# Strided sparse attention with a feed-forward block on one core: scores of two heads or slots from one full-row matmul with a block-diagonal query tile

## The chip, the core and the metric

One of the eight cores of a Trainium2 chip runs the whole program. The metric is the device time in microseconds of one execution, as the median of several runs; smaller is better. The engines named below are PE (TensorE, the matrix engine), ACT (ScalarE), DVE (VectorE), POOL (GpSimd, here only the issuer of loads) and SP (here only the issuer of stores). PSUM is the memory that matmuls write, in eight banks; SBUF is the memory that everything else is in.

## What is computed

For 8 batches of 8 heads, 576 positions and head size 64, attention with two fixed sparse masks, and then a feed-forward layer with a squared ReLU over all 4608 tokens:

```python
scores = scale * np.matmul(q, k.transpose(0, 1, 3, 2))
mask_local   = (rel >= 0) & (rel < 32)                                        # heads 0 to 3
mask_strided = (rel >= 0) & (pos[None, :] % 32 == pos[:, None] % 32)          # heads 4 to 7
attn = softmax(np.where(masks, scores, -1e9));   x = np.matmul(attn, v)
h = x @ w_in;  r = np.maximum(h, 0.0)
out = (s * (r * r) + b) @ w_out            # x: 4608 x 512, w_in: 512 x 2048, w_out: 2048 x 512
```

Since the masks are sparse, a local head needs only six blocks of 96 queries against 128 keys, and a strided head only eight blocks ("slots") of 72 queries against 72 keys.

## The kernel before, in words

**Attention of a batch.** `load_qk` and `load_v` (lines 100 to 136) load a batch through POOL's queue. The heads are worked on in four pairs, m = 0 and 1 local, m = 2 and 3 strided. `pair_steps` (line 149) makes five lists of steps for a pair, each step with one matmul:

- T (`trans`, line 160): transposes of q and then of k into a PSUM tile `ps_t` (two buffers). The last transpose of each is followed by a copy on ACT into SBUF, 128 rows by 576 columns (line 180 for local pairs, 185 for strided). In the copy, two heads (local) or two neighbouring slots of a head (strided) lie one above the other: rows 0 to 63 and rows 64 to 127.
- S (`score`, line 196): the scores. Each matmul contracts over 64 rows, one head or slot, and gives keys by 96 (or 72) queries: 12 matmuls for a local pair and 16 for a strided one. Neighbouring steps use the upper and the lower 64 rows in turn. Three of them fill a PSUM tile `ps_s` (two buffers); then ACT takes the exponential of 288 columns (line 211) and DVE multiplies by the mask (line 216).
- A0 and A1 (`av`, line 227): probabilities times values for the first and the second head, 6 (local) or 8 (strided) matmuls each. A column of ones beside v gives the sums; after 6 (local) or 4 (strided) matmuls DVE takes reciprocals (line 240) and scales into `x_nat` (line 242). The PSUM tile `ps_a` has one buffer, so the next group of A steps has to wait until line 242 has read it.
- X (`xtrans`, line 252): transposes of `x_nat` into `xT`, the input of the feed-forward layer.

`batch_steps` (line 274) puts the lists of the four pairs in one sequence, in phases: in a phase the T steps of a pair stand in alternating halves with the S steps of the pair before it, followed by the A0 steps of the pair before that, X of the pair before that, and A1. X of the last pair is kept apart.

**Feed-forward of a block.** A block is 512 tokens, and there are nine (T = 0 to 8). FF1 is 64 matmuls of 512 columns into `ps_f` (three buffers); after every fourth, ACT takes the ReLU into `u` (line 307) and DVE squares it into `gT` (line 308). FF2 is another 64 matmuls; after every 16th DVE makes the output (line 322) and SP stores it. In block 0 a group of 16 matmuls (line 340) that needs `w_out` stands between FF1 and FF2.

**The order.** It is written out by hand and every engine works in program order. Batch 0 runs alone. Then block T carries the attention of batch T + 1 among its own 128 matmuls: step i of the sequence stands ahead of feed-forward matmul number int(i * 112 / len(seq)), and X of the last pair stands at numbers 118 to 120. Blocks 0 to 6 carry attention, blocks 7 and 8 none. The two lines that place the steps are:

```python
for i, f in enumerate(seq):
    at.setdefault(int(i * 112 / len(seq)), []).append(f)
```

Of the kernel before, what the change touches and what calls it, by code (L numbers as in the profile page):

```python
# [9 lines left out]
FP16 = mybir.dt.float16  # L10
FP32 = mybir.dt.float32
AF = mybir.ActivationFunctionType
ALU = mybir.AluOpType
# [3 lines left out]
def kernel(  # L17
# [11 lines left out]
    nc = tc.nc  # L29
    B, H, S, D = q.shape  # L30
# [3 lines left out]
    scale = 1.0 / float(np.sqrt(D))  # L34
# [6 lines left out]
    LQ, LT, LPAD = 96, 6, 32  # L41
    SQ, ST = 72, 8
# [13 lines left out]
    const = ctx.enter_context(tc.tile_pool(name="consts", bufs=1))  # L56
    inp = ctx.enter_context(tc.tile_pool(name="inp", bufs=2))
    qkp = ctx.enter_context(tc.tile_pool(name="qkp", bufs=2))
    ptp = ctx.enter_context(tc.tile_pool(name="ptp", bufs=8))
# [4 lines left out]
    op = ctx.enter_context(tc.tile_pool(name="op", bufs=3))  # L64
    psum = ctx.enter_context(tc.tile_pool(name="psum", bufs=1, space=bass.MemoryType.PSUM))
# [11 lines left out]
    v_loc = [const.tile([128, 4, LT, D + 1], FP16, name=f"v_loc{i}") for i in range(NV)]  # L77
    v_str = [const.tile([SQ, 4, ST, D + 1], FP16, name=f"v_str{i}") for i in range(NV)]
    kT_loc = [const.tile([128, LPAD + S], FP16, name=f"kT_loc{i}") for i in range(2)]
    xT = [const.tile([128, NTOK], FP16, name=f"xT{i}") for i in range(4)]  # L80

    sched = ctx.enter_context(tc.manual_schedule())
# [11 lines left out]
        nc.vector.memset(v_str[i][:, :, :, D:D + 1], 1.0)  # L94
    for i in range(2):
        nc.vector.memset(kT_loc[i][:, 0:LPAD], 0.0)

    loaded = {}

# [49 lines left out]
    def pair_steps(b, m):  # L149

        loc = m < 2
        nq, nt = (LQ, LT) if loc else (SQ, ST)
        sfx = "l" if loc else "s"
        mm = m % 2
        half = nt // 2
        nk = 128 if loc else SQ
        st = {}
        T, SS, A0, A1, X = [], [], [], [], []

        def trans(name, j):  # L160
            def f():
                if j == 0:
                    st["p" + name] = psum.tile([128, S], FP16, tag="t", bufs=2, name="ps_t")
                ps = st["p" + name]

                src = (paired[b, name][:, mm, j] if loc else
                       loaded[b][name + sfx][:, 2 * mm + j // 4,
                                             (j % 4) * 128:(j % 4) * 128 + 128])
                nc.tensor.matmul(  # L169
                    out=ps[:, nq * j:nq * j + nq], lhsT=src,  # L170
                    rhs=ident[0:nq, 0:nq], is_transpose=True)
                if j == nt - 1:
                    if loc:
                        if name == "q":
                            st["q"] = qkp.tile([128, S], FP16, tag="qTl", name="qTl")
                            dst = st["q"]
                        else:
                            st["k"] = kT_loc[mm]
                            dst = st["k"][:, LPAD:LPAD + S]
                        nc.scalar.copy(  # L180
                            out=dst.rearrange("d (p j) -> d p j", j=nt),
                            in_=ps.rearrange("d (j p) -> d p j", j=nt))
                    else:
                        st[name] = qkp.tile([128, S], FP16, tag=name + "Ts", name=name + "Ts")
                        nc.scalar.copy(out=st[name], in_=ps)  # L185
            return f

        for name in ("q", "k"):
            for j in range(nt):
                T.append(trans(name, j))  # L190

        def grp(j):

            return (j // half, j % half) if loc else (j % 2, j // 2)

        def score(e, j):
            def f():
                g, i = grp(j)
                if i == 0:
                    st["s", e, g] = psum.tile([128, 3 * LQ], FP32, tag="s", bufs=2, name="ps_s")  # L200
                ps = st["s", e, g]
                c = i * nq
                r0, at = (64 * e, j * nq) if loc else (64 * (j % 2), (4 * e + j // 2) * nq)
                rr = slice(r0, r0 + 64)
                nc.tensor.matmul(  # L205
                    out=ps[0:nk, c:c + nq], lhsT=st["k"][rr, at:at + nk],
                    rhs=st["q"][rr, at:at + nq])
                if i == half - 1:
                    pt = ptp.tile([128, half, nq], FP16, tag="pt" + sfx, name="pt")
                    st["pt", e, g] = pt  # L210
                    nc.scalar.activation(  # L211
                        out=pt[0:nk].rearrange("k t c -> k (t c)"),
                        in_=ps[0:nk, 0:half * nq], func=AF.Exp, scale=scale)
                    mask = (mask_loc if loc else mask_str)[:, None, :].to_broadcast(
                        [nk, half, nq])
                    nc.vector.tensor_tensor(out=pt[0:nk], in0=pt[0:nk], in1=mask, op=ALU.mult)  # L216
            return f

        for a in range(2):
            for j in range(half):  # L220
                for c in range(2):
                    SS.append(score(c, a * half + j) if loc else score(a, 2 * j + c))

        per = nt if loc else nt // 2
        vt = (v_loc if loc else v_str)[b % NV]

        def av(e, j):
            def f():
                if j == 0 and e == 0:
                    st["x"] = xnp.tile([nq, nt, 128], FP16, tag="x" + sfx, name="x_nat")  # L230
                if j % per == 0:
                    st["a"] = psum.tile([128, 6, D + 1], FP32, tag="a", bufs=1, name="ps_a")
                ps = st["a"]
                nc.tensor.matmul(  # L234
                    out=ps[0:nq, j % per, :],
                    lhsT=st["pt", e, grp(j)[0]][0:nk, grp(j)[1], :],
                    rhs=vt[0:nk, 2 * mm + e, j, :])
                if j % per == per - 1:
                    rec = recp.tile([128, 6, 1], FP32, tag="rec", name="rec")
                    nc.vector.reciprocal(out=rec[0:nq, 0:per], in_=ps[0:nq, 0:per, D:D + 1])  # L240
                    j0 = j - per + 1
                    nc.vector.tensor_tensor(  # L242
                        out=st["x"][:, j0:j0 + per, 64 * e:64 * e + 64],
                        in0=ps[0:nq, 0:per, 0:D],
                        in1=rec[0:nq, 0:per].to_broadcast([nq, per, D]), op=ALU.mult)
            return f

        for j in range(nt):
            A0.append(av(0, j))
            A1.append(av(1, j))  # L250

        def xtrans(j):
            def f():
                if j == 0:
                    st["px"] = psum.tile([128, S], FP16, tag="t", bufs=2, name="ps_t")
                ps = st["px"]
                nc.tensor.matmul(  # L257
                    out=ps[:, nq * j:nq * j + nq], lhsT=st["x"][:, j, :],
                    rhs=ident[0:nq, 0:nq], is_transpose=True)
                if j == nt - 1:  # L260
                    dst = xT[m][:, b * S:(b + 1) * S]
                    if loc:
                        nc.vector.tensor_copy(out=dst, in_=ps)
                    else:
                        nc.scalar.copy(  # L265
                            out=dst.rearrange("d (p j) -> d p j", j=nt),
                            in_=ps.rearrange("d (j p) -> d p j", j=nt))
            return f

        for j in range(nt):  # L270
            X.append(xtrans(j))
        return T, SS, A0, A1, X

    def batch_steps(b):

        P = [pair_steps(b, m) for m in range(4)]
        seq = []
        for ph in range(6):
            Tn = P[ph][0] if ph < 4 else []
            Sn = P[ph - 1][1] if 0 <= ph - 1 < 4 else []  # L280
            seq += Sn[:len(Sn) // 2] + Tn[:len(Tn) // 2] + Sn[len(Sn) // 2:] + Tn[len(Tn) // 2:]
            if 0 <= ph - 2 < 4:
                seq += P[ph - 2][2]
            if 0 <= ph - 3 < 4:
                seq += P[ph - 3][4]
            if 0 <= ph - 2 < 4:
                seq += P[ph - 2][3]
        return seq, P[3][4]
# [67 lines left out]
    for T in range(NBLK):  # L356
        F = ffn_steps(T)
        at = {}
# [46 lines left out]
```

## Time and profile before

| | us |
|---|---|
| median of 3 runs (lowest to highest) | 461.65 (460.33 to 464.23) |
| the profiled execution, its own time | 465.23 |
| its span, first to last instruction | 463.5 |
| PE busy in the span | 393.1 |
| ACT busy | 177.7 |
| DVE busy | 198.6 |

The profiled execution is 3.6 us longer than the median of the runs, and 1.7 us of its time lie outside the span. In the trace a PE instruction's duration covers the filling and emptying of the array too, and matmuls overlap, so what one costs the engine is read from the distance between starts and not from its duration.

### The profile page before, as it was taken

The page shows a single profiled execution, that of the slowest core. Times are in us where ns is not written, and L with a number is a line of the kernel's source. Part 1 is how long each engine was busy: PE and PEld are TensorE (multiplying, and loading weights), DVE is VectorE, ACT ScalarE, POOL GpSimd, SP SyncE. Part 2 cuts the span into 40 slices and gives each one's busy share as a digit, 9 for nine tenths or more (in the row PEclk, how much of TensorE's full clock was granted, in tenths as well). Part 3 has the DMA queues.
Part 4 walks back from the last instruction along what each step waited for, and adds up shares of the span by engine and source line. Part 5 has one row for each costly group of instructions (what it writes and reads, how often), then busy time and mean ns, then how long its engine had stood idle before and what let it go on. Part 6 is the DMA issues. An engine that isn't in the chain of part 4 may idle for free.

```text
span 463.5 us, 6912 instructions
## 1 busy us (share of the span) xinstructions
PE 393.1 (85%) x2736; PEld 194.7 (42%) x2736; DVE 198.6 (43%) x557; ACT 177.7 (38%) x354; POOL 100.1 (22%) x137
## 2 busy tenths in 40 slices
PE   1848799788978989788978898888969797999995
PEld 0633344344434444344434343444434343444442
DVE  1552434444453444434444444434444355352431
ACT  2614651065503751065414651166305541260530
POOL 6736436510244012510252022400000000000000
PEclk9999999899999999899999999899999999899999
DMA  8999999960567114850458025700001001101101
GB/s 108 93 204 100 164 156 141 88 103 1 60 75 87 32 25 60 68 102 0 61 75 119 1 30 67 82 24 1 24 24 45 1 0 47 45 2 46 47 23 69
DMA packets 72516, 28.99 MB, mean 63 GB/s; under 512 B 53028, under 2 KB 67876, under 8 KB 72484
## 3 DMA queue, kind: packets, MB, share of 16 engines
q0 software_dynamic: 66640, 19.04, 44.1%
q1 hardware_dynamic: 5844, 9.51, 5.6%
q8 instruction: 21, 0.34, 0.3%
q14 instruction: 11, 0.09, 0.1%
HBM read 38.08 MB, written 9.44 MB: 103 GB/s over the span
## 4 chain that ended last, share of the span: by engine, by line
PE 71%; DVE 9%; ACT 7%; DMA 6%; issue 3%; POOL 2%; ACTq 0%; POOLq 0%
PE ps_f L302 27%; PE ps_f L317 26%; PE ps_s L205 9%; DVE x_nat L242 5%; PE ps_a L234 4%; ACT u L307 4%; DMA kl<-in_k_dram 3%; PE ps_t L169 3%; DMA qs<-in_q_dram 2%; ACT kT_loc L180 2%; DVE rec L240 2%; PE ps_t L257 1%; DVE o L322 1%; DVE gT L308 1%; ACT kTs L185 1%
## 5 line engine op out<-in xcount | busy, mean ns | idle before, releaser
L302 PE MATMUL ps_f<-xT,w_in_sb 128*128 128x512 f16 x576 | 178.2, 388 | 0.0
L317 PE MATMUL ps_f<-w_out_sb,gT 128*128 128x512 f16 x576 | 166.9, 393 | 0.0
L307 ACT ACTIVATE u<-ps_f 128x512 f16<-128x512 f32 x144 | 86.0, 597 | 72.9 <-PE ps_f L302 72.3
L308 DVE TENSOR_TENSOR gT<-u 128x512 f16<-128x512 f16 x144 | 61.3, 426 | 109.2 <-ACT u L307 109.2
L317 PEld LDWEIGHTS <-gT 128*128 128x128 f16 x576 | 58.0, 102 | 39.1 <-issue 4.3
L234 PEld LDWEIGHTS <-pt 72*72 72x72 f16 (+1 forms) x448 | 44.1, 127 | 71.3 <-DVE x_nat L242 58.3
L211 ACT ACTIVATE pt<-ps_s 72x288 f16<-72x288 f32 (+1 forms) x128 | 48.2, 407 | 59.8 <-PE ps_s L205 58.4
L302 PEld LDWEIGHTS <-w_in_sb 128*128 128x128 f16 x576 | 56.8, 99 | 33.4 <-issue 0.6
L234 PE MATMUL ps_a<-v_str,pt 72*72 72x65 f16 x256 | 39.1, 211 | 29.1 <-DVE x_nat L242 28.8
L265 ACT COPY xT<-ps_t 128x576 f16<-128x576 f16 x16 | 10.2, 639 | 108.6 <-PE ps_t L257 108.6
L242 DVE TENSOR_TENSOR x_nat<-ps_a,rec 72x256 f16<-72x256 f32 (+1 forms) x96 | 44.6, 465 | 3.3
L322 DVE SCALAR_TENSOR_TENSOR o<-ps_f,s_sb,bcs 128x512 f32<-128x512 f32 x36 | 26.9, 747 | 37.1 <-PE ps_f L317 37.1
L134 POOL DMA_DIRECT2D v_str<-in_v_dram x32 | 28.0, 875 | 65.5 <-PE ps_a L234 45.4
L240 DVE RECIPROCAL rec<-ps_a 72x4 f32<-72x4 f32 (+1 forms) x96 | 17.4, 181 | 53.3 <-PE ps_a L234 52.5
L234 PE MATMUL ps_a<-v_loc,pt 128*96 128x65 f16 x192 | 27.3, 209 | 13.2 <-DVE x_nat L242 13.2
L205 PE MATMUL ps_s<-qTl,kT_loc 64*128 64x96 f16 x192 | 26.3, 221 | 11.3 <-ACT kT_loc L180 11.3
L205 PE MATMUL ps_s<-qTs,kTs 64*72 64x72 f16 x256 | 34.4, 222 | 0.8 <-ACT pt L211 0.5
L205 PEld LDWEIGHTS <-kTs 64*72 64x72 f16 x256 | 16.6, 112 | 33.1 <-issue 32.8
L257 PE MATMUL ps_t<-ident,x_nat 72*128 72x72 f16 (+1 forms) x224 | 29.9, 215 | 0.5 <-DVE x_nat L242 0.5
L133 POOL DMA_DIRECT2D v_loc<-in_v_dram x32 | 28.7, 898 | 6.1 <-DVE x_nat L242 2.3
L216 DVE TENSOR_TENSOR pt<-pt,mask_str 72x288 f16<-72x288 f16 x64 | 19.0, 304 | 25.2 <-ACT pt L211 25.1
L205 PEld LDWEIGHTS <-kT_loc 64*128 64x128 f16 x192 | 11.6, 95 | 40.2 <-issue 23.5
(37 smaller groups left out, 251.3 us busy)
## 6 DMA issues: line engine op xcount, KB each, us to landing
out_dram<-o SPq DMA_DIRECT2D x36, 256.0 KB, 2.1
v_loc<-in_v_dram POOLq DMA_DIRECT2D x32, 80.0 KB, 3.5
ql<-in_q_dram POOLq DMA_DIRECT2D x8, 288.0 KB, 5.3
kl<-in_k_dram POOLq DMA_DIRECT2D x8, 288.0 KB, 6.2
qs<-in_q_dram POOLq DMA_DIRECT2D x8, 288.0 KB, 6.6
ks<-in_k_dram POOLq DMA_DIRECT2D x8, 288.0 KB, 8.1
v_str<-in_v_dram POOLq DMA_DIRECT2D x32, 72.0 KB, 3.6
w_in_sb<-in_moe_w_in_dram POOLq DMA_DIRECT2D x4, 512.0 KB, 9.7
```

The source lines that it names most:

```text
L133: nc.gpsimd.dma_start(out=vl[:, h, 1:LT, 0:D], in_=src)
L134: nc.gpsimd.dma_start(out=vs[:, h, :, 0:D], in_=v[b, 4 + h].rearrange("(p j) d -> p j d", j=ST))
L205: nc.tensor.matmul(out=ps[0:nk, c:c + nq], lhsT=st["k"][rr, at:at + nk], rhs=st["q"][rr, at:at + nq])
L211: nc.scalar.activation(out=pt[0:nk].rearrange("k t c -> k (t c)"), in_=ps[0:nk, 0:half * nq], func=AF.Exp, scale=scale)
L234: nc.tensor.matmul(out=ps[0:nq, j % per, :], lhsT=st["pt", e, grp(j)[0]][0:nk, grp(j)[1], :], rhs=vt[0:nk, 2 * mm + e, j, :])
L242: nc.vector.tensor_tensor(out=st["x"][:, j0:j0 + per, 64 * e:64 * e + 64], in0=ps[0:nq, 0:per, 0:D], in1=rec[0:nq, 0:per].to_broadcast([nq ...
L257: nc.tensor.matmul(out=ps[:, nq * j:nq * j + nq], lhsT=st["x"][:, j, :], rhs=ident[0:nq, 0:nq], is_transpose=True)
L302: nc.tensor.matmul(out=st["h"], lhsT=w_in_sb[:, ct, ft * 128:(ft + 1) * 128], rhs=xT[ct][:, tok0:tok0 + PS], start=(ct == 0), stop=(ct == 3))
L307: nc.scalar.activation(out=u, in_=st["h"], func=AF.Relu)
L308: nc.vector.tensor_tensor(out=st["g"][:, ft, :], in0=u, in1=u, op=ALU.mult)
L317: nc.tensor.matmul(out=st["o"], lhsT=st["g"][:, ft, ts * 128:(ts + 1) * 128], rhs=w_out_sb[:, ft, :], start=(ft == 0), stop=(ft == NFT - 1))
L322: nc.vector.scalar_tensor_tensor(out=o, in0=st["o"], scalar=s_sb[:, 0:1], in1=bcs, op0=ALU.mult, op1=ALU.add)
```

## The change

The q copy of a pair no longer goes into one dense tile. It goes into a tile `qD_loc` or `qD_str` that holds, for each block of queries, twice as many columns: in the first half of the columns only rows 0 to 63 are filled, in the second half only rows 64 to 127, and the rest is zero. These tiles are zeroed once, at the start, by DVE, and the zeros are never overwritten. ACT copies the upper 64 rows and DVE the lower 64. A score step is now one matmul over all 128 rows: 192 columns (local) or 144 columns (strided), and it gives the scores of both heads or slots. There are half as many score steps, 6 or 8 to a pair; two (local) or three (strided) of them fill a `ps_s` tile, so the exponential and the mask now work on 384, 432 or (last group of a strided pair) 288 columns. The k copies, the transposes and the A and X steps are as before, except for where A finds its probabilities.

```diff
+    qD_loc = [const.tile([128, LT, 2, LQ], FP16, name=f"qD_loc{i}") for i in range(2)]
+    qD_str = [const.tile([128, ST, 2, SQ], FP16, name=f"qD_str{i}") for i in range(2)]
...
     for i in range(2):
         nc.vector.memset(kT_loc[i][:, 0:LPAD], 0.0)
+        nc.vector.memset(qD_loc[i], 0.0)
+        nc.vector.memset(qD_str[i], 0.0)
...
-                        if name == "q":
-                            st["q"] = qkp.tile([128, S], FP16, tag="qTl", name="qTl")
-                            dst = st["q"]
...
-                        st[name] = qkp.tile([128, S], FP16, tag=name + "Ts", name=name + "Ts")
-                        nc.scalar.copy(out=st[name], in_=ps)
+                    if name == "q":
+                        qD = (qD_loc if loc else qD_str)[mm]
+                        st["q"] = qD
+                        for e, copy in ((0, nc.scalar.copy), (1, nc.vector.tensor_copy)):
+                            hs = slice(64 * e, 64 * e + 64)
+                            if loc:
+                                copy(out=qD[hs, :, e, :].rearrange("d t (p j) -> d t p j", j=nt),
+                                     in_=ps[hs].rearrange("d (j t p) -> d t p j", j=nt, t=nt))
+                            else:
+                                copy(out=qD[hs, :, e, :],
+                                     in_=ps[hs].rearrange("d (j p) -> d j p", j=nt))
...
-                r0, at = (64 * e, j * nq) if loc else (64 * (j % 2), (4 * e + j // 2) * nq)
-                rr = slice(r0, r0 + 64)
-                nc.tensor.matmul(
-                    out=ps[0:nk, c:c + nq], lhsT=st["k"][rr, at:at + nk],
-                    rhs=st["q"][rr, at:at + nq])
-                if i == half - 1:
+        per_s = 2 if loc else 3
+
+        def score(i):
+            def f():
+                g, n = i // per_s, min(per_s, nt - i // per_s * per_s)
+                if i % per_s == 0:
+                    st["s", g] = psum.tile([128, 3 * 2 * SQ], FP32, tag="s", bufs=2, name="ps_s")
...
+                c = i % per_s * 2 * nq
+                nc.tensor.matmul(
+                    out=ps[0:nk, c:c + 2 * nq], lhsT=st["k"][:, i * nq:i * nq + nk],
+                    rhs=st["q"][:, i].rearrange("d e c -> d (e c)"))
+                if i % per_s == n - 1:
...
-        for a in range(2):
-            for j in range(half):
-                for c in range(2):
-                    SS.append(score(c, a * half + j) if loc else score(a, 2 * j + c))
+        for i in range(nt):
+            SS.append(score(i))
```

The placed sequence of a batch has 160 steps in place of 188, so the other steps move too: 1.43 steps stand ahead of each of the first 112 feed-forward matmuls of a block in place of 1.68.

On PE, block 3, in FF1, where the first scores of batch 4 follow the k transposes of its first pair (`ps_f` rows are feed-forward, `ps_s` rows scores); before:

```order
L302 LDWEIGHTS w_in_sb
L302 MATMUL ps_f<-xT_102,w_in_sb 128x512
L205 LDWEIGHTS kT_loc_98
L205 MATMUL ps_s<-qTl,kT_loc_98 128x96
L205 LDWEIGHTS kT_loc_98
L205 MATMUL ps_s<-qTl,kT_loc_98 128x96
L302 LDWEIGHTS w_in_sb
L302 MATMUL ps_f<-xT_103,w_in_sb 128x512
```

The same place after the change, where line 313 is the FF1 matmul and line 213 the score:

```order
L313 LDWEIGHTS w_in_sb
L313 MATMUL ps_f<-xT_107,w_in_sb 128x512
L213 LDWEIGHTS kT_loc_98
L213 MATMUL ps_s<-qD_loc_100,kT_loc_98 128x192
L313 LDWEIGHTS w_in_sb
L313 MATMUL ps_f<-xT_104,w_in_sb 128x512
L213 LDWEIGHTS kT_loc_98
L213 MATMUL ps_s<-qD_loc_100,kT_loc_98 128x192
```

A place between two feed-forward matmuls that held one or two scores of 96 columns holds one or two of 192, and there are fewer such places.

On PE, block 3, in FF2, where the first group of four A steps of pair 2 (`ps_a`) ends and the second group begins; before:

```order
L317 LDWEIGHTS gT
L317 MATMUL ps_f<-w_out_sb,gT 128x512
L234 LDWEIGHTS pt
L234 MATMUL ps_a<-v_str_96,pt 72x65
L234 LDWEIGHTS pt
L234 MATMUL ps_a<-v_str_96,pt 72x65
L317 LDWEIGHTS gT
L317 MATMUL ps_f<-w_out_sb,gT 128x512
```

The first of these two A matmuls is the group's last and the second begins the next group. After the change (line 328 is the FF2 matmul, line 245 the A matmul):

```order
L245 LDWEIGHTS pt
L245 MATMUL ps_a<-v_str_96,pt 72x65
L328 LDWEIGHTS gT
L328 MATMUL ps_f<-w_out_sb,gT 128x512
L245 LDWEIGHTS pt
L245 MATMUL ps_a<-v_str_96,pt 72x65
```

A feed-forward matmul now stands between the end of the one group and the start of the other.

On ACT, in FF1 of a block, from the first q copy of a batch on (`u` is the ReLU, `pt` the exponential); before:

```order
L180 COPY qTl<-ps_t 128x576
L307 ACTIVATE u<-ps_f 128x512
L180 COPY kT_loc_98<-ps_t 128x576
L307 ACTIVATE u<-ps_f 128x512
L211 ACTIVATE pt<-ps_s 128x288 x2
L307 ACTIVATE u<-ps_f 128x512
L180 COPY qTl<-ps_t 128x576
```

The same place after the change:

```order
L184 COPY qD_loc_100<-ps_t 64x6x96
L318 ACTIVATE u<-ps_f 128x512
L191 COPY kT_loc_98<-ps_t 128x576
L318 ACTIVATE u<-ps_f 128x512
L219 ACTIVATE pt<-ps_s 128x384
L318 ACTIVATE u<-ps_f 128x512
L184 COPY qD_loc_101<-ps_t 64x6x96
```

The order of ACT's work stays; the exponentials become fewer and wider, and the q copy has half the rows and as many columns.

## Rows read from the trace of the kernel before

**Rows 1.** The page: busy time and instructions, then the granted clock in 40 slices.

```profile
PE 393.1 (85%) x2736; PEld 194.7 (42%) x2736; DVE 198.6 (43%) x557; ACT 177.7 (38%) x354; POOL 100.1 (22%) x137
...
PEclk9999999899999999899999999899999999899999
```

**Rows 2.** Busy time by stretch: FF1, FF2 of block 3; FF2 of block 4; blocks 7, 8.

```profile
core 0: us, PE busy (x) PEld busy (x) DVE busy (x) ACT busy (x) POOL busy (x), PEclk, DMA share, GB/s
...
198.50:224.90 26.40, 23.41 (x175) 11.42 (x174) 11.53 (x32) 16.77 (x35) 0.72 (x1) 1.00 0.25 39
224.90:249.10 24.20, 20.44 (x156) 10.32 (x155) 11.76 (x35) 3.97 (x8) 11.12 (x15) 1.00 0.68 80
...
275.40:300.80 25.40, 21.85 (x156) 10.83 (x155) 11.79 (x35) 4.00 (x8) 9.77 (x13) 0.93 0.63 75
403.00:458.00 55.00, 55.00 (x256) 24.92 (x255) 19.64 (x40) 19.11 (x32) 0.00 (x0) 1.00 0.10 39
```

**Rows 3.** Timeline of PE in FF1 of block 3: start us, us, engine, line, operation.

```profile
199.93 0.25 PE L169 MATMUL ps_t<-ident,kp 96*128 96x96 f16 x2
200.01 0.38 PE L302 MATMUL ps_f<-xT,w_in_sb 128*128 128x512 f16 x1
200.23 0.21 PE L169 MATMUL ps_t<-ident,kp 96*128 96x96 f16 x1
200.28 0.38 PE L302 MATMUL ps_f<-xT,w_in_sb 128*128 128x512 f16 x1
...
201.32 0.39 PE L302 MATMUL ps_f<-xT,w_in_sb 128*128 128x512 f16 x1
201.64 0.22 PE L205 MATMUL ps_s<-qTl,kT_loc 64*128 64x96 f16 x2
201.79 0.39 PE L302 MATMUL ps_f<-xT,w_in_sb 128*128 128x512 f16 x1
202.11 0.21 PE L205 MATMUL ps_s<-qTl,kT_loc 64*128 64x96 f16 x1
202.26 0.39 PE L302 MATMUL ps_f<-xT,w_in_sb 128*128 128x512 f16 x1
```

**Rows 4.** The score line alone: what ended its engine's idle time (us, times).

```profile
  issue: 56.3, 242
```

**Rows 5.** Waits of PE over the span: us in total, times, longest us.

```profile
PE ps_a L234 <- DVE x_nat L242: 42.0, 56, 1.6
PE ps_s L205 <- ACT kT_loc L180: 11.3, 16, 0.9
```

**Rows 6.** Timeline of PE in block 3, first A matmuls of groups in FF2.

```profile
234.49 0.22 PE L234 MATMUL ps_a<-v_str,pt 72*72 72x65 f16 x1 [0.73 <-DVE x_nat L242]
...
237.68 0.26 PE L234 MATMUL ps_a<-v_str,pt 72*72 72x65 f16 x2 [0.51 <-DVE x_nat L242]
```

**Rows 7.** Timeline of all engines in FF1 of block 3, between A0 and A1.

```profile
216.49 0.23 PE L234 MATMUL ps_a<-v_loc,pt 128*96 128x65 f16 x1 [1.56 <-DVE x_nat L242]
```

**Rows 8.** Groups by shape: busy us, mean ns of one, idle before and releaser.

```profile
L307 ACT ACTIVATE u<-ps_f 128x512 f16<-128x512 f32 x144 | 86.0, 597 | 72.9 <-PE ps_f L302 72.3
...
L242 DVE TENSOR_TENSOR x_nat<-ps_a,rec 72x256 f16<-72x256 f32 x64 | 26.9, 420 | 2.2
...
L211 ACT ACTIVATE pt<-ps_s 128x288 f16<-128x288 f32 x64 | 24.3, 411 | 10.9 <-PE ps_s L205 10.4
...
L242 DVE TENSOR_TENSOR x_nat<-ps_a,rec 96x384 f16<-96x384 f32 x32 | 17.7, 554 | 1.1
...
L180 ACT COPY qTl<-ps_t 128x576 f16<-128x576 f16 x16 | 10.2, 638 | 17.5 <-PE ps_t L169 17.4
...
L263 DVE COPY xT<-ps_t 128x576 f16<-128x576 f16 x16 | 7.2, 451 | 3.6 <-PE ps_t L257 3.5
...
L121 DVE COPY qp<-ql 96x768 f16<-96x768 f16 x16 | 4.9, 349 | 4.4 <-DMA ql<-in_q_dram 4.4
...
L93 DVE MEMSET v_loc<- 32x260 f16 x2 | 0.6, 275 | 0.2
```

**Rows 9.** The tile `w_out_sb`: duration ns min/median/max, first and last start us.

```profile
L340 PE MATMUL ps_f<-w_out_sb,ones x16: 379/379/381, 66.0 to 69.2; 128*128 128x512 f16 x16
L145 POOL DMA_DIRECT2D w_out_sb<-in_moe_w_out_dram x1: 1179/1179/1179, 45.1 to 45.1; - x1
...
DMA to landing us min/median/max: 15.9/15.9/15.9
```

More of the change, by code (lines that the diff above doesn't have):

```diff
@@ L172, in f @@
                 if j == nt - 1:
-                    if loc:
-                        if name == "q":
-                            st["q"] = qkp.tile([128, S], FP16, tag="qTl", name="qTl")
-                            dst = st["q"]
-                        else:
-                            st["k"] = kT_loc[mm]
-                            dst = st["k"][:, LPAD:LPAD + S]
+                    if name == "q":
[9 more added lines that the diff above has]
+                                     in_=ps[hs].rearrange("d (j p) -> d j p", j=nt))
+                    elif loc:
+                        st["k"] = kT_loc[mm]
                         nc.scalar.copy(
-                            out=dst.rearrange("d (p j) -> d p j", j=nt),
+                            out=kT_loc[mm][:, LPAD:LPAD + S].rearrange("d (p j) -> d p j", j=nt),
                             in_=ps.rearrange("d (j p) -> d p j", j=nt))
                     else:
-                        st[name] = qkp.tile([128, S], FP16, tag=name + "Ts", name=name + "Ts")
-                        nc.scalar.copy(out=st[name], in_=ps)
+                        st["k"] = qkp.tile([128, S], FP16, tag="kTs", name="kTs")
+                        nc.scalar.copy(out=st["k"], in_=ps)
             return f
@@ L190, in pair_steps @@
                 T.append(trans(name, j))
-        def grp(j):
-            return (j // half, j % half) if loc else (j % 2, j // 2)
-        def score(e, j):
+        per_s = 2 if loc else 3
+        def score(i):
             def f():
[L198 to L202, printed above, removed]
-                r0, at = (64 * e, j * nq) if loc else (64 * (j % 2), (4 * e + j // 2) * nq)
-                rr = slice(r0, r0 + 64)
-                nc.tensor.matmul(
-                    out=ps[0:nk, c:c + nq], lhsT=st["k"][rr, at:at + nk],
-                    rhs=st["q"][rr, at:at + nq])
-                if i == half - 1:
-                    pt = ptp.tile([128, half, nq], FP16, tag="pt" + sfx, name="pt")
-                    st["pt", e, g] = pt
+                g, n = i // per_s, min(per_s, nt - i // per_s * per_s)
+                if i % per_s == 0:
+                    st["s", g] = psum.tile([128, 3 * 2 * SQ], FP32, tag="s", bufs=2, name="ps_s")
+                ps = st["s", g]
+                c = i % per_s * 2 * nq
+                nc.tensor.matmul(
+                    out=ps[0:nk, c:c + 2 * nq], lhsT=st["k"][:, i * nq:i * nq + nk],
+                    rhs=st["q"][:, i].rearrange("d e c -> d (e c)"))
+                if i % per_s == n - 1:
+                    pt = ptp.tile([128, 2 * per_s, nq], FP16, tag="pt" + sfx, name="pt")
+                    st["pt", g] = pt
@@ L211, in f @@
                     nc.scalar.activation(
-                        out=pt[0:nk].rearrange("k t c -> k (t c)"),
-                        in_=ps[0:nk, 0:half * nq], func=AF.Exp, scale=scale)
+                        out=pt[0:nk, 0:2 * n].rearrange("k t c -> k (t c)"),
+                        in_=ps[0:nk, 0:2 * n * nq], func=AF.Exp, scale=scale)
                     mask = (mask_loc if loc else mask_str)[:, None, :].to_broadcast(
-                        [nk, half, nq])
-                    nc.vector.tensor_tensor(out=pt[0:nk], in0=pt[0:nk], in1=mask, op=ALU.mult)
@@ L217, in score, with p_of @@
-            return f
-        for a in range(2):
-            for j in range(half):
-                for c in range(2):
-                    SS.append(score(c, a * half + j) if loc else score(a, 2 * j + c))
+                        [nk, 2 * n, nq])
+                    nc.vector.tensor_tensor(
+                        out=pt[0:nk, 0:2 * n], in0=pt[0:nk, 0:2 * n], in1=mask, op=ALU.mult)
+            return f
+        for i in range(nt):
+            SS.append(score(i))
+        def p_of(e, j):
+            i, r = (j, e) if loc else (4 * e + j // 2, j % 2)
+            return st["pt", i // per_s][0:nk, i % per_s * 2 + r, :]
@@ L235, in f @@
                     out=ps[0:nq, j % per, :],
-                    lhsT=st["pt", e, grp(j)[0]][0:nk, grp(j)[1], :],
+                    lhsT=p_of(e, j),
                     rhs=vt[0:nk, 2 * mm + e, j, :])
```

## The prediction

> **What bounds the kernel now.** I read the page first, then the busy time by stretch, then PE's timeline in one block, then its waits, and at last the groups by shape for the prices. PE is busy for 85% of the span and ACT and DVE for well under half [rows 1], so PE's program is the path in the blocks. How much of PE's time is work shows against blocks 7 and 8, which carry no attention: 256 feed-forward matmuls in 55.0 us, 0.215 us each [rows 2]. FF1 of block 3 has 64 of them, 13.8 us of 26.4; the other 12.6 us are attention and waits, and in FF2 it is 10.4 of 24.2 [rows 2].
>
> PE's timeline shows where they go [rows 3]. With transposes between, feed-forward matmuls run on: 200.01 to the transpose at 200.23 is 0.22 us, and the transpose of 96 columns adds 0.05. With scores between it is another picture. From the feed-forward matmul at 201.32 to the scores at 201.64 are 0.32 us, from there to the next feed-forward matmul at 201.79 are 0.15: 0.47 us in all, 0.255 more than 0.215. A single score costs the same as two (202.11 to 202.26 is 0.15 as well): the two of a visit run side by side, and the price is one of the visit. Before a score the weight loader is idle with nothing that the profile shows as the cause, 242 times, 56.3 us in all, 0.23 each [rows 4]. In the order of the instructions there are 36 such visits in each of blocks 0 to 6, 252 in all. At 0.255 us they take 64 us.
>
> The score is the only matmul here that contracts over 64 rows. Transposes over 96 rows do not show the gap [rows 3], nor do the A matmuls over 72. I take the gap to belong to going from 128 rows to 64 and back. The Trainium skill says so in its own terms (TensorEngine Tiling (Array Packing), Key Properties: changing the tiling mode drains the engine). No run here has yet shown a score without it.
>
> **The change, part by part.**
>
> *Scores.* 392 score matmuls in the seven blocks become 196: 84 of 192 columns and 112 of 144. No row shows these widths. 96 columns cost 0.045 and 512 cost 0.215 [rows 2, 3], so 0.41 ns a column: 0.084 and 0.064 us, 7.1 + 7.2 = 14.3 us. If the gap goes, the term is 14.3 - 64.3 = -50.0 us. The bound from below is 1 us better (no fixed part); the bound from above, the gap staying, is rival 2.
>
> *A groups.* PE waits 42.0 us, 56 times, for the single `ps_a` buffer [rows 5]. Step i stands at number int(i * 112 / 188) before and int(i * 112 / 160) after. Each block has five places in FF2 where one strided group follows the next directly. At three of them no feed-forward matmul stands between now; afterwards one stands at all five. With one the idle time is 0.51, without 0.73 [rows 6]: three times 0.22, seven blocks, -4.6 us. In FF1, between A0 and A1 of the first pair, PE idles 1.56 us [rows 7], because DVE's scaling stands behind the square of a ReLU group, and that ReLU behind a k copy. Now the group ends with matmul 39 and A0's last step stands at number 41, two later; afterwards the group ends with 35 and A0 at 39, four later, so the square is done some 0.44 us earlier, and A1's first step comes one feed-forward matmul later at most. I take -0.6 us a block, -4.2 us, with 0 and -7 as bounds.
>
> *k copies.* Scores wait for k's copy 16 times, 0.7 us each [rows 5]; copy and queue stay as they are. I take 0, with 0.3 us either way for the 14 in the blocks, so -4 to +4 us.
>
> *q copies.* ACT's half has as many columns as before, and I take the same 0.638 us [rows 8]; nothing there grows. DVE gets four more copies a batch. A dense copy from PSUM of this width takes 0.451; at the rate of the scaling, which goes from 0.420 for 256 to 0.554 for 384 columns, 576 would take 0.755 [rows 8]. That is 1.8 to 3.0 us a block, on an engine busy 23 of 51 us [rows 2], and the fused masks give some back. It is hidden behind the k transposes and the 4 to 6 feed-forward matmuls among them, all of which stand between the q transposes and the first score; without that cover it is rival 4.
>
> *Exponentials.* Per batch 16 of 0.41 become six of 384, four of 432 and two of 288 columns. From 0.411 for 288 to 0.597 for 512 columns [rows 8] these take 0.49, 0.53 and 0.41: 6.6 us become 5.9. ACT is off the path, so 0.
>
> *Zeroing.* Four tiles of 1152 columns. A zeroing of 260 columns takes 0.275 [rows 8], so at its worst rate 1.2 us each, 4.9 us; if written in words of twice the size, half. DVE otherwise idles until the first q arrives, part of the 4.4 us ahead of line 121 [rows 8]. I take 0, with +1 as the bound.
>
> *Batch 0 and block 0.* Batch 0 runs alone, waiting for loads and for one engine after another; its 56 scores become 28 wider ones. I take 0, with 1 us either way. In block 0 the matmuls with `w_out` start at 66.0; that load is issued at 45.1 and lands 15.9 us later, at about 61 [rows 9]. FF1 there would now end at about 61 too: 1 us of the gain is lost.
>
> *Clock.* FF2 of block 4 has granted clock 0.93 and lasts 25.4 us, that of block 3 has 1.00 and lasts 24.2 [rows 2]: a stretch at 1.2 GHz costs 1.2 us. The page's clock row shows at least four slices with a dip after the start [rows 1]. I count them as staying; all gone would be -6, one in every block +2.
>
> *Sum.* -50.0 - 4.6 - 4.2 + 1 = -57.8 us; I keep -57. The profiled execution's 465.2 us become 408.2, and since it lies 3.6 us above the median of the runs, the forecast is 404.6 us, told as 405. By the bounds that aren't rivals (k copies 4, A0/A1 3 to 4, clock 2 to 6, the rest 2), taken together in part, its own range is 395 to 414. FF1 of a block should fall to about 21 us and FF2 to about 21.5.
>
> **Rivals.**
>
> *1. ACT becomes the bound in FF1.* It is busy 16.8 of 26.4 us there [rows 2]. After the change its 16 ReLUs, 8 copies and 9 exponentials have 9.6 + 5.1 + 4.4 = 19.1 us of durations, to fit in 21. For it: everything is in order, and the k copies and the ReLUs that free `ps_f` stand in one queue. Against it: the same sum now is 19.6 and shows as 16.8 busy, since instructions overlap; and `ps_f` has three buffers. If FF1 cannot go below these 19.1 us plus the waits between (two for k, 1.4, and the 1.56 of A), it ends at 22.1 to 23.5, in the worse case 2.3 us a block later than forecast: 16 us, so 421.
>
> *2. The gap is not of the row count.* It stays with every visit. The order now has 154 visits, with 42 scores beside a first one: 154 x (0.255 + 0.04) + 42 x 0.074 = 48.5 us in place of 64.3, which with the A groups and block 0 gives -24: 438. Against it: rows over 72 and 96 run without.
>
> *3. Side-by-side scores were the cheaper form.* Two scores of 64 rows start together [rows 3], so a pair streams in the time of one: 84 x 0.045 + 112 x 0.035 = 7.7 us, against 14.3 after. The Trainium skill's advice goes this way (TensorEngine Tiling (Array Packing), When to Use Tiling and Theoretical Speedup: contraction up to 64 is worth twofold row tiling, up to twice as fast). By that alone, with the time of the gaps taken up by something else, the change costs 6.6 us: 468, slower. It decides only if the 64 us are no drain at all, and the 0.15 us of a visit with one score speaks against it.
>
> *4. DVE's half of q comes late.* DVE's queue holds squares that wait for ReLUs; a q copy behind them could be as late as the scaling in FF1 is, 1.56 us, plus its own 0.755 [rows 7, 8]: 28 pairs at 2.3 us are 65 us, so 469, slower. It decides from 57 / 28 = 2.0 us of wait at each pair. Against it: about 1.2 to 1.9 us of other PE work stands between, so less than 1 us would show.
>
> **How the numbers follow.** Forecast 0.71, rival 1 0.16, rival 2 0.08, rival 3 0.02, rival 4 0.02, and 0.01 for no change at all. The range takes in the forecast's own range and most of rival 1: 394 to 423. One percent, 4.6 us, is about what a measurement tells from no change. Faster 0.95, same 0.01, slower 0.04.
>
> **What would show it.** In the changed profile, scores should start 0.22 us after the feed-forward matmul ahead of them and the next one follow 0.06 to 0.09 later, and the score line's idle time without a cause should go. FF1 near 21 with PE's waits on k copies at 0.7 shows the sum right; FF1 near 23 with waits on ReLUs or longer ones on k copies shows rival 1; 0.32 before scores shows rival 2; waits of scores on a DVE copy show rival 4. FF2 above 22.5 without a clock dip would say that the A groups gave nothing. The prediction is wrong if the gap is still there.

## The result, and the profile after

The changed kernel takes 408.37 us (median of 4 runs, 407.28 to 411.25) against 460.99 for the kernel before (459.26 to 464.23): a ratio of 0.886, 95% interval 0.879 to 0.893. It is faster, and the forecast of 405 us lies 0.8% under the measured time. Ratios and intervals, here and below, compare fast runs of the two kernels; for the last two experiments, beside which fast runs of the kernel before spread from 459.1 to 464.4 us, the record calls the verdict unclear.

The page of the changed kernel, to be laid beside [rows 1]; its line 313 is the FF1 matmul (302 before), 328 FF2 (317), 213 the score (205), 245 the A step (234), 253 the scaling (242), 333 the output (322):

```profile
PE 333.7 (82%) x2512; PEld 184.2 (45%) x2512; DVE 215.1 (53%) x561; ACT 169.7 (42%) x322; POOL 100.1 (25%) x137
...
PEclk9999999999999999999999999999999999999998
```

PE lost 59 us of busy time and 224 instructions, DVE gained 17 us (20 for its half of the q copies and 2 for the zeroing, less what the wider masks save), and the clock row has lost its dips but for the last slice, where PE is done. The stretches that answer to [rows 2] are block 0's FF1 and FF2, FF1 and FF2 of block 3, and blocks 7 and 8:

```profile
35.30:62.60 27.30, 24.58 (x173) 13.25 (x172) 13.87 (x36) 17.37 (x34) 13.00 (x18) 1.00 1.54 145
62.60:84.20 21.60, 17.85 (x143) 9.74 (x142) 11.23 (x32) 3.43 (x6) 14.51 (x20) 1.00 1.70 143
171.10:192.60 21.50, 18.66 (x159) 10.80 (x158) 13.42 (x33) 16.17 (x32) 1.33 (x2) 1.00 0.27 45
192.60:214.60 22.00, 17.93 (x143) 9.61 (x142) 11.67 (x34) 3.47 (x7) 10.52 (x15) 1.00 0.77 91
345.00:400.00 55.00, 55.00 (x256) 24.95 (x255) 19.61 (x40) 19.10 (x32) 0.00 (x0) 1.00 0.10 39
```

FF1 went from 26.4 to 21.5 us and FF2 from 24.2 to 22.0. The two blocks without attention are as before. PE's timeline, where [rows 3] had 0.32 us ahead of scores and 0.15 behind them:

```profile
175.83 0.25 PE L213 MATMUL ps_s<-qD_loc,kT_loc 128*128 128x192 f16 x1
175.91 0.38 PE L313 MATMUL ps_f<-xT,w_in_sb 128*128 128x512 f16 x1
176.13 0.24 PE L213 MATMUL ps_s<-qD_loc,kT_loc 128*128 128x192 f16 x1
176.21 0.38 PE L313 MATMUL ps_f<-xT,w_in_sb 128*128 128x512 f16 x1
```

Now 0.22 us lie between a feed-forward matmul and the score behind it, and 0.08 between that and the next. The score line's idle time without a cause, 56.3 us in 242 places in [rows 4], is gone:

```profile
  issue: 0.7, 2
```

The waits of PE that answer to [rows 5] have not gone down:

```profile
PE ps_a L245 <- DVE x_nat L253: 44.4, 57, 1.4
PE ps_s L213 <- ACT kT_loc L191: 12.0, 16, 1.1
```

The prices that the prediction had to bound, in the groups by shape:

```profile
L219 ACT ACTIVATE pt<-ps_s 128x384 f16<-128x384 f32 x48 | 22.4, 486 | 5.6 <-PE ps_s L213 4.7
...
L184 DVE COPY qD_loc<-ps_t 64x576 f16<-64x576 f16 x16 | 12.2, 761 | 7.8 <-ACT qD_loc L184 7.7
...
L184 ACT COPY qD_loc<-ps_t 64x576 f16<-64x576 f16 x16 | 10.1, 632 | 16.7 <-PE ps_t L174 16.6
...
L187 DVE COPY qD_str<-ps_t 64x576 f16<-64x576 f16 x16 | 7.4, 460 | 2.0 <-ACT qD_str L187 0.8
```

ACT's copy of half the rows takes what the whole copy took; DVE's takes 0.76 where the source is strided and 0.46 where it is dense, about the two ends of the range given.

### The profile page after: what moved, and what is told of

Read it like the earlier page. It is cut to its first block, busy times and chain, and to the rows that moved or that the text cites. A ratio compares the mean times of both kernels' runs of the same rounds, so it can differ in the third digit from the quotient of the medians.

```text
span 405.5 us, 6454 instructions
## 1 busy us (share of the span) xinstructions
PE 333.7 (82%) x2512; PEld 184.2 (45%) x2512; DVE 215.1 (53%) x561; ACT 169.7 (42%) x322; POOL 100.1 (25%) x137
## 4 chain that ended last, share of the span: by engine, by line
PE 58%; ACT 18%; DVE 15%; issue 6%; DMA 2%; POOL 0%; ACTq 0%; POOLq 0%
PE ps_f L328 26%; PE ps_f L313 18%; ACT u L318 9%; DVE x_nat L253 7%; PE ps_a L245 6%; ACT pt L219 4%; PE ps_s L213 4%; DVE o L333 3%; PE ps_t L174 2%; DVE rec L251 2%; ACT kT_loc L191 2%; DVE gT L319 2%; DMA kl<-in_k_dram 2%; PE ps_t L268 1%; ACT qD_str L187 1%
## 5 line engine op out<-in xcount | busy, mean ns | idle before, releaser
L313 PE MATMUL ps_f<-xT,w_in_sb 128*128 128x512 f16 x576 | 159.0, 383 | 0.0
L328 PE MATMUL ps_f<-w_out_sb,gT 128*128 128x512 f16 x576 | 151.0, 380 | 0.0
L328 PEld LDWEIGHTS <-gT 128*128 128x128 f16 x576 | 56.1, 99 | 44.0
L219 ACT ACTIVATE pt<-ps_s 128x384 f16<-128x384 f32 (+2 forms) x96 | 44.8, 486 | 31.2 <-PE ps_s L213 29.0
L276 ACT COPY xT<-ps_t 128x576 f16<-128x576 f16 x16 | 10.2, 639 | 109.9 <-PE ps_t L268 109.9
L245 PE MATMUL ps_a<-v_loc,pt 128*96 128x65 f16 x192 | 29.4, 208 | 13.5 <-DVE x_nat L253 13.5
L213 PE MATMUL ps_s<-qD_loc,kT_loc 128*128 128x192 f16 x96 | 21.5, 265 | 12.0 <-ACT kT_loc L191 12.0
L213 PE MATMUL ps_s<-qD_str,kTs 128*72 128x144 f16 x128 | 23.4, 238 | 0.3 <-ACT pt L219 0.3
L268 PEld LDWEIGHTS <-x_nat 72*128 72x128 f16 (+1 forms) x224 | 19.2, 103 | 9.6 <-DVE x_nat L253 0.7
L114 POOL DMA_DIRECT2D qs<-in_q_dram x8 | 5.9, 743 | 70.8 <-PE ps_t L174 70.8
L224 DVE TENSOR_TENSOR pt<-pt,mask_loc 128x384 f16<-128x384 f16 x48 | 16.4, 356 | 11.9 <-ACT pt L219 11.4
```

Source lines behind the costliest of these rows:

```text
L213: nc.tensor.matmul(out=ps[0:nk, c:c + 2 * nq], lhsT=st["k"][:, i * nq:i * nq + nk], rhs=st["q"][:, i].rearrange("d e c -> d (e c)"))
L219: nc.scalar.activation(out=pt[0:nk, 0:2 * n].rearrange("k t c -> k (t c)"), in_=ps[0:nk, 0:2 * n * nq], func=AF.Exp, scale=scale)
L245: nc.tensor.matmul(out=ps[0:nq, j % per, :], lhsT=p_of(e, j), rhs=vt[0:nk, 2 * mm + e, j, :])
L268: nc.tensor.matmul(out=ps[:, nq * j:nq * j + nq], lhsT=st["x"][:, j, :], rhs=ident[0:nq, 0:nq], is_transpose=True)
L313: nc.tensor.matmul(out=st["h"], lhsT=w_in_sb[:, ct, ft * 128:(ft + 1) * 128], rhs=xT[ct][:, tok0:tok0 + PS], start=(ct == 0), stop=(ct == 3))
L328: nc.tensor.matmul(out=st["o"], lhsT=st["g"][:, ft, ts * 128:(ts + 1) * 128], rhs=w_out_sb[:, ft, :], start=(ft == 0), stop=(ft == NFT - 1))
```

## The experiments

Theory 1 is the prediction's: the gap of 0.255 us a visit belongs to going from matmuls over 128 rows to matmuls over 64 and back. Its rival, theory 2: the gain comes from fewer and wider score steps and the placement that follows from their number. The first two runs change one of the two each. Theory 3 concerns the term that the profile shows to have failed, the A groups.

**Full rows, nothing fused.** The scores are those of the kernel before in number, width and place, but over 128 rows of the new tile, whose two half copies of q, one on ACT and one on DVE, come with it:

```diff
-                r0, at = (64 * e, j * nq) if loc else (64 * (j % 2), (4 * e + j // 2) * nq)
-                rr = slice(r0, r0 + 64)
+                blk, r = (j, e) if loc else (4 * e + j // 2, j % 2)
                 nc.tensor.matmul(
-                    out=ps[0:nk, c:c + nq], lhsT=st["k"][rr, at:at + nk],
-                    rhs=st["q"][rr, at:at + nq])
+                    out=ps[0:nk, c:c + nq], lhsT=st["k"][:, blk * nq:blk * nq + nk],
+                    rhs=st["q"][:, blk, r, :])
```

> The kernel before with only the row count of the scores changed: each score matmul contracts over all 128 rows of the zero-filled query tile, but still gives one head's or slot's 96 or 72 columns, so there are 56 score steps a batch, the 188-step placement and the exponentials of 288 columns as before. Theory 1 (the gap of 0.255 us a visit belongs to going between 64 and 128 rows): the gap goes, 392 scores cost 168 x 0.045 + 224 x 0.035 = 15.4 us in place of 64, so about 461 - 49 = 412, and scores start 0.22 us after the feed-forward matmul. Theory 2 (fewer and wider score steps and the new placement bring the gain): 455 to 461, with 0.32 us ahead of scores.

Measured: 415.59 us, ratio to before 0.902 (0.896 to 0.907). Its PE timeline in FF1 of block 3, and the score line's idle time without a cause:

```profile
178.33 0.25 PE L215 MATMUL ps_s<-qD_loc,kT_loc 128*128 128x96 f16 x2
178.41 0.38 PE L315 MATMUL ps_f<-xT,w_in_sb 128*128 128x512 f16 x1
178.63 0.21 PE L215 MATMUL ps_s<-qD_loc,kT_loc 128*128 128x96 f16 x1
178.67 0.38 PE L315 MATMUL ps_f<-xT,w_in_sb 128*128 128x512 f16 x1
```

```profile
  issue: 1.2, 5
```

0.22 ahead of a score, and 0.04 for each of 96 columns: the two of a visit no longer run side by side (0.08 for two), and it does not matter. Scores over twice the rows, half of them zeros, are worth 45 us of the 53 by themselves, the new q copies included.

**Fused steps, 64 rows.** The kernel before, with the two side-by-side scores in one step, so that the placement is the changed kernel's:

```diff
-                for c in range(2):
-                    SS.append(score(c, a * half + j) if loc else score(a, 2 * j + c))
+                pr = [score(c, a * half + j) if loc else score(a, 2 * j + c) for c in range(2)]
+                SS.append(lambda pr=pr: [g() for g in pr])
```

> The kernel before with only the placement changed: the two scores of 64 rows that run side by side stand in one step, so a batch has the changed kernel's 160 steps and 154 visits in the seven blocks. Theory 1: every visit still costs 0.255 us, 39 us where the changed kernel's scores cost 14.3, so about 408 + 25 = 433, and up to 6 more if the clock dips come back. Theory 2 (placement and number of steps bring the gain): about 408.

Measured: 437.32 us, ratio 0.948 (0.944 to 0.953). The timeline and the score line's idle time without a cause:

```profile
188.99 0.39 PE L302 MATMUL ps_f<-xT,w_in_sb 128*128 128x512 f16 x1
189.32 0.22 PE L205 MATMUL ps_s<-qTl,kT_loc 64*128 64x96 f16 x2
189.47 0.39 PE L302 MATMUL ps_f<-xT,w_in_sb 128*128 128x512 f16 x1
```

```profile
  issue: 35.2, 151
```

The price of a visit is unchanged, 0.33 + 0.15, and there are 151 of them in place of 242, at 0.23 us each as before; the time lies within theory 1's 433 to 439. The four kernels make a table (medians, us):

| | 188 steps a batch | 160 steps a batch |
|---|---|---|
| scores over 64 rows | 460.99 | 437.32 |
| scores over 128 rows | 415.59 | 408.37 |

Rows alone give 45, placement alone 24, both together 53: with the gap gone there is little left for fewer visits to save. Theory 1 stands; theory 2 explains 7 us once the rows are full. Which half of the rows a score uses does not matter: in the trace of the kernel before, visits of a single score cost 0.32 and 0.15 us on rows 0 to 63 as on rows 64 to 127 (medians over 35 of each).

**Two buffers for the A groups.** The tiles take all eight banks of PSUM (two `ps_t`, two `ps_s`, one `ps_a`, three `ps_f`), so `ps_t` has one buffer in place of two:

```diff
-tag="a", bufs=1    tag="t", bufs=2
+tag="a", bufs=2    tag="t", bufs=1
```

> The changed kernel with two buffers for ps_a and one for ps_t (PSUM is full). Theory 3 (the waits of A steps for the single ps_a, 44 us idle in all, lie on the path, and the A groups are where the forecast was too hopeful): A waits all but go, 6.5 us a block, and the single ps_t costs some 2 us a block back, so about 408 - 30 = 378, between 370 and 395. Rival: the waits hide something else (DVE or ACT would be late anyway), so 403 to 410; or the single ps_t eats it all, 410 to 425.

Measured: 392.04 us, ratio 0.849 (0.845 to 0.853). FF1 and FF2 of block 3, and PE's waits:

```profile
165.40:189.50 24.10, 18.97 (x158) 10.70 (x156) 13.39 (x33) 16.54 (x32) 1.26 (x2) 1.00 0.28 43
189.50:206.40 16.90, 16.90 (x143) 9.93 (x142) 11.47 (x34) 3.53 (x7) 11.22 (x15) 1.00 0.91 109
```

```profile
PE ps_t L174 <- DVE qD_loc L184: 19.3, 16, 3.5
PE ps_t L174 <- DVE qD_str L187: 12.2, 16, 1.0
```

FF2 falls from 22.0 to 16.9 us, and PE is busy without a break there. FF1 rises by 2.6, because the k transposes now wait for DVE's half of the q copy, 31.5 us in all. The time is within the range expected but 14 us over its centre: with the A wait of 1.4 us in FF1 gone as well, the single `ps_t` costs 4 us a block, where 2 was put. So the A waits were on the path, and DVE's half of q is late enough to cost as soon as a second `ps_t` does not cover it: this is the mechanism of rival 4 of the prediction, seen at another wait.

**The output later.** DVE's output operation is issued four feed-forward matmuls after its group ends:

```diff
-                    o = op.tile([128, DM], FP32, tag="o", name="o")
-                    nc.vector.scalar_tensor_tensor(
+                    def evac():
+                        o = op.tile([128, DM], FP32, tag="o", name="o")
+                        nc.vector.scalar_tensor_tensor(
...
+                    late.append([4 if (T, ts) != (NBLK - 1, 3) else 0, evac])
```

> The changed kernel with the output operation of DVE (0.75 us each) issued four feed-forward matmuls later. Theory 3a (the A groups gave nothing because the new placement puts the output operation just ahead of the reciprocal of two groups a block, whose waits are 1.4 and 1.05 us where the others are 0.67): both fall to about 0.67, 1.1 us a block, 7 blocks, so about 400.5. Rival: the output only moves to another wait, or the length of the chain and not the queue sets these waits: 406 to 409.

Measured: 401.54 us, ratio 0.870 (0.865 to 0.874), 6.8 us under the changed kernel. In the changed kernel, DVE at the first strided group of block 3 and PE behind it:

```profile
198.21 0.74 DVE L333 SCALAR_TENSOR_TENSOR o<-ps_f,s_sb,bcs 128x512 f32<-128x512 f32 x1
198.87 0.17 DVE L251 RECIPROCAL rec<-ps_a 72x4 f32<-72x4 f32 x1
```

```profile
199.55 0.22 PE L245 MATMUL ps_a<-v_str,pt 72*72 72x65 f16 x1 [1.25 <-DVE x_nat L253]
...
202.96 0.22 PE L245 MATMUL ps_a<-v_str,pt 72*72 72x65 f16 x1 [0.51 <-DVE x_nat L253]
...
206.30 0.26 PE L245 MATMUL ps_a<-v_str,pt 72*72 72x65 f16 x2 [0.88 <-DVE x_nat L253]
```

The reciprocal stands right behind the output (and that behind two masks), and the wait is 1.25 us; at 206.30 the output is ahead again, and it is 0.88; where nothing is in the way it is 0.51. With the output moved, the same two waits in its run:

```profile
197.66 0.22 PE L245 MATMUL ps_a<-v_str,pt 72*72 72x65 f16 x1 [0.60 <-DVE x_nat L253]
...
204.03 0.26 PE L245 MATMUL ps_a<-v_str,pt 72*72 72x65 f16 x2 [0.51 <-DVE x_nat L253]
```

**The second `ps_a` paid for by `ps_s`.**

```diff
-tag="a", bufs=1    tag="s", bufs=2
+tag="a", bufs=2    tag="s", bufs=1
```

> The changed kernel with two buffers for ps_a, paid for with one for ps_s. The A waits go as in the run with a single ps_t (FF2 from 21.8 to about 16.6 us). Theory: a single ps_s makes the second and third group of each pair wait for the exponential before them, about 0.6 us in 8 places a block, 4 to 5 us, of which 1.2 in FF2; so FF1 24 to 25, FF2 18, 392 to 400. Rival: with the wide groups the scores stand far enough apart that one buffer is enough, 375 to 382.

Measured: 407.23 us, ratio 0.884 (0.880 to 0.888), slower than expected. The A waits go, and scores wait for the exponential instead:

```profile
PE ps_s L213 <- ACT pt L219: 44.0, 64, 1.3
```

64 places at 0.69 us, where 0.6 in eight places a block was expected; FF2 is 18.0 us long, as expected, and FF1 25.5, over the 24 to 25. The cost is as high as what the A waits gave. By its own lengths of FF1 and FF2, 42 to 43 us a block against 43.5 in the changed kernel, the expectation should have said 398 to 405.

**The second `ps_a` paid for by `ps_f`.**

```diff
-tag="a", bufs=1    tag="f", bufs=3
+tag="a", bufs=2    tag="f", bufs=2
```

> The changed kernel with two buffers for ps_a, paid for with two in place of three for ps_f. This tests rival 1 of the prediction from the other side: if ACT's queue is near its limit in FF1, a group of four feed-forward matmuls (1.15 us with what stands between) does not cover the ReLU (0.6 us) behind copies and exponentials, and FF1 grows by 2 to 5 us a block: 390 to 410. If ACT has room, FF1 stays near 20 and FF2 falls to 16.6: 370 to 376.

Measured: 368.48 us, ratio 0.800 (0.796 to 0.803), better than the better expectation. FF1 and FF2 of block 3:

```profile
156.90:177.30 20.40, 18.70 (x159) 10.86 (x157) 13.55 (x33) 16.37 (x32) 1.58 (x3) 1.00 0.31 50
177.30:194.20 16.90, 16.90 (x144) 9.93 (x143) 11.29 (x33) 3.34 (x6) 10.95 (x14) 1.00 0.94 112
```

In FF1 ACT is busy 16.4 of 20.4 us, and with two `ps_f` buffers no wait for a ReLU is among PE's waits: the third was nearly idle reserve (FF1 of blocks 7 and 8, without attention, is 14.0 us each in place of 13.8). Rival 1 is out.

**The k copies covered.** Each phase begins with the next pair's q transposes:

```diff
-            seq += Sn[:len(Sn) // 2] + Tn[:len(Tn) // 2] + Sn[len(Sn) // 2:] + Tn[len(Tn) // 2:]
+            seq += Tn[:len(Tn) // 2] + Sn[:len(Sn) // 2] + Tn[len(Tn) // 2:] + Sn[len(Sn) // 2:]
```

> The changed kernel with each phase beginning with the q transposes of the next pair in place of the scores, so that a k copy is covered by them. Theory: the wait of the first score for the k copy (12.0 us idle, 16 times; two a block of 0.7 and 1.1 us) is on the path and goes, 1.8 us a block: FF1 from 21.4 to about 19.6, 408 - 12.5 = 396. Rival: ACT's and DVE's queues are what FF1 waits for and the time turns up as a longer wait of A steps, 404 to 409.

Measured: 402.86 us, ratio 0.874 (0.870 to 0.877), 5.5 under the changed kernel, half of what was expected. The wait for the k copy is gone from the list, and FF1 of blocks 1 to 6 is 20.0 us in place of 21.5. Block 0 takes part of it back: the `w_out` matmuls behind its FF1 wait for their load.

```profile
34.90:66.80 31.90, 25.46 (x173) 13.44 (x172) 14.10 (x36) 17.06 (x34) 14.27 (x19) 0.89 1.54 143
```

```profile
PE ps_f L351 <- DMA w_out_sb<-in_moe_w_out_dram: 5.0, 1, 5.0
```

Block 0's FF1, the `w_out` matmuls with it, is 31.9 us long in place of 27.3, with the clock at 0.89.

**Both.** The two edits above that gave most, two `ps_a` with two `ps_f`, and the k copies covered:

> The changed kernel with two ps_a and two ps_f buffers and with the k copies covered by the next pair's q transposes. If the waits of A steps and of the first scores are separate parts of PE's path, the gains add up: 368.5 - 5.5 to 368.5 - 10 = 358 to 363, FF1 near 19, FF2 near 16.6. If ACT's queue comes in (two ps_f and no pauses any more), FF1 stays at 20.4 and the time at 367 to 369.

Measured: 359.33 us, ratio 0.777 (0.771 to 0.784). The gains add up, 40 and 5.5 us against 49. Most of the rest is in block 0, whose FF1 with the `w_out` matmuls is held up once and not twice: 30.8 us, where the two runs have 30.5 and 31.9 and the changed kernel 27.3. In block 3 FF1 takes 18.8 us, 18.5 of them PE's, and waits for a ReLU show for the first time:

```profile
152.80:171.60 18.80, 18.48 (x158) 10.97 (x157) 13.11 (x32) 15.71 (x32) 2.04 (x4) 1.00 0.36 59
```

```profile
PE ps_f L313 <- ACT u L318: 1.1, 7, 0.2
```

This is the fastest version tried.

**The q copy on ACT alone.**

```diff
-for e, copy in ((0, nc.scalar.copy), (1, nc.vector.tensor_copy)):
+for e, copy in ((0, nc.scalar.copy), (1, nc.scalar.copy)):
```

> The changed kernel with both halves of the q copy on ACT, so that DVE has four copies a batch less (2.4 us) and ACT four more (2.1 to 2.5 us). The prediction's reading, that DVE's half is hidden and no score waits for it: 406 to 411, and if ACT's queue reaches the k copies, up to 3 us more. Rival 4's reading, that DVE's copy is a cost on the path: 400 to 405.

Measured: 435.00 us, ratio 0.940 (0.931 to 0.949): neither expectation, 27 us slower than the changed kernel. Its waits, FF1 of block 3 and the clock row:

```profile
PE ps_a L245 <- DVE x_nat L253: 53.7, 57, 2.0
PE ps_s L213 <- ACT kT_loc L191: 22.5, 16, 1.8
```

```profile
181.70:206.90 25.20, 20.25 (x158) 11.48 (x157) 10.59 (x27) 18.12 (x35) 1.28 (x2) 0.93 0.24 37
```

```profile
PEclk9999999998999989998999999998999899999999
```

Four more copies a batch on ACT delay the k copies (22.5 in place of 12.0 us) and, through ReLU and square, the scaling (53.7 in place of 44.4). That is 20 us; the stretches at 1.2 GHz, one in FF1 of each of blocks 1 to 6, are the likely source of the rest (six at the 1.2 us of the prediction make 7), which no run isolates. So ACT has room for its own work in FF1, and none for the other half of q.

## Why the prediction came out right

*The gap.* The chief step, that the gap belongs to going from 128 rows to 64 and back, held, and the first two runs isolate it. Of -50.0 us, 7.14 a block, the trace shows about as much: block 3, which had no clock dip before, went from 50.6 us (198.5 to 249.1) to 43.5 (171.1 to 214.6), 7.1 less, with all waits about 0.3 us longer, so about 7.4 for the scores. Two scores of 64 rows did run side by side, but it did not pay here, because what stood around them on PE was 128 rows and each visit cost 0.255 us. So the up to twofold gain that the Trainium skill names for a contraction of up to 64 (TensorEngine Tiling (Array Packing), Theoretical Speedup), on which rival 3 rested, was a loss in this order. By the Trainium skill a change of tiling mode drains the engine (TensorEngine Tiling (Array Packing), Key Properties). All four kernels of the table agree: the idle time without a cause stands ahead of 242 and 151 visits with scores over 64 rows, and in 5 and 2 places with scores over 128.

*Widths.* 0.084 and 0.064 us a score were forecast; 0.083 is the median distance from a 192-column score to the next matmul and 0.063 that from a 144-column one, worked out over all of them from the starts in the trace.

*A groups: the term that failed.* -4.6 and -4.2 us were forecast. PE's waits for `ps_a` are 4.1 us in FF2 of block 3 where they were 3.7, and 1.4 between A0 and A1 where they were 1.6. In place of -8.8 us the term is +1.4, seven times 0.2.

In FF2, "afterwards one stands at all five" was true, but the step from it to "three times 0.22" was not. I had followed PE's order at these places and not DVE's. Before, the output operation stood ahead of one of the five reciprocals, and PE waited 1.10 us there and not the 0.73 that I took:

```profile
239.54 0.22 PE L234 MATMUL ps_a<-v_str,pt 72*72 72x65 f16 x1 [1.10 <-DVE x_nat L242]
```

The new placement put it just ahead of two others, with waits of 1.25 and 0.88. The run with the late output shows that this queue cost 6.8 of the 10.2 us by which the term was short.

Between A0 and A1, most of the 0.6 forecast was a square done 0.44 us earlier. It was not: from A0's last step to A1's first are 1.79 us where 1.76 were, and the wait fell by 0.2 only because a feed-forward matmul now stands between the two. The ReLU ahead of that square starts when ACT has done the k copy, and not when its own matmuls end; ACT works there without idle time from 181.70 to 185.18 us:

```profile
183.45 0.64 ACT L196 COPY kTs<-ps_t 128x576 f16<-128x576 f16 x1
183.97 1.21 ACT L318 ACTIVATE u<-ps_f 128x512 f16<-128x512 f32 x2
```

The sign that the prediction named for this, FF2 above 22.5, did not show: FF2 took 22.0 with the A groups giving nothing. The sign was set too high.

*Clock: a term that I left at 0.* It gave about what the A groups did not: before, the clock had five stretches at 1.2 GHz in FF2 after the start, at about 1.2 us each, 6 us; afterwards it has none. (Four are to be seen in [rows 1]; the fifth, in FF2 of block 1 with a granted clock of 0.93, falls across two slices.) That is the end of the range that the prediction named for "all gone". Full rows alone removed them too, and with 64 rows and the new placement one stayed, in block 6. What made these stretches go is seen in no more detail than that. That this gain and the loss in the A groups nearly cancel is luck.

*Hidden costs.* ACT's copy (0.632 against 0.638), DVE's (0.76 and 0.46 against 0.451 to 0.755), the exponentials (0.486 for 384 columns against 0.49) and the zeroing (the first FF1 matmul at 35.3 us in place of 35.2) came out as forecast. The 1 us for `w_out` in block 0 was not due: the load was issued 1.5 us earlier, and PE's weight loader waited 0.2 us for it. Block 0 gave 10.7 us where 7.4 was forecast (7.1 for the scores and 1.3 for the A groups, less 1). Of that, 1.2 are a clock dip. Another 1.9 are the clock's first rise to 2.4 GHz, 3.8 us sooner: from the start of a 512-column matmul to the next instruction are 0.42 us up to 41.0 us and 0.22 from there, where before the same step came at 44.8.

*The sum.* From execution to execution, 408.2 us was forecast and 407.3 was measured: -57 against -58. As measured, the scores gave -52 (7.4 a block), the waits +2, the clock stretches -6 and the sooner rise -1.9. That the forecast of the median was 3.4 us low comes from another step: I moved it by the 3.6 us that the profiled execution of the kernel before lay above its median, and the one after lies 1.1 us below its own.

*Rivals.* Rival 2, the gap staying, and rival 3, slower, are refuted by the trace and by both runs that isolate the rows. Rival 1 is refuted by the run with two `ps_f`; the terms named for it add up to 22.1 us in FF1, and nothing in them gives the 23.5 and the 421. Rival 4 did not happen: scores did not wait for DVE. But the late copies behind it are there, as the run with one `ps_t` shows.

## What to carry to other kernels

Before packing small matmuls into half the array's rows, look at what stands around them: among full-row matmuls each visit of half-row ones cost 0.255 us here, and filling the other half with zeros was worth more than running two at once. When steps are placed by their number, a change in the number moves every one of them past the others: follow the order on the engine that releases a wait (here DVE's output ahead of a reciprocal), not only on the one that waits. And where a wait for a single buffer adds up, look for a tile with a buffer to spare: trading one of three `ps_f` for a second `ps_a` gave 40 us, while trading one of `ps_s` gave nothing.

## What was not expected of the hardware

Four more copies of 0.63 us a batch on ACT, 20 us of work over the whole program on an engine that is busy 42% of it, made the program 27 us longer. PE's waits account for 20 of them; the same run had a stretch at 1.2 GHz in FF1 of each of blocks 1 to 6, as the rows show for block 3 (granted clock 0.93 over 25.2 us), where the changed kernel has none. Whether the longer waits brought those stretches about, no run here shows: the run with one `ps_s` buffer has 44 us of waits on scores and none.
